# MoE slots per expert cut from 640 to 624 in a fused attention and mixture-of-experts kernel

## Chip, cores and metric

One Trainium2 chip, one core, one launch. The metric is the device time of the launch in microseconds, as the median of the runs shown. TensorE is called PE, VectorE DVE, ScalarE ACT, GpSimd POOL and SyncE SP, as in the profile.

## What is computed

The reference is rotary attention on 4 sequences of 576 tokens with 8 heads of 64, whose output becomes 2304 rows of 512, followed by a mixture of 8 experts with two experts per row:

```python
logits = x @ w_gate
noise_scale = np.log1p(np.exp(x @ w_noise))
noisy_logits = logits + noise_scale * noise
top2 = np.argpartition(-noisy_logits, 2, axis=1)[:, :2]
# top2_w: softmax over the two chosen logits
for e in range(E):
    for k in range(2):
        mask = top2[:, k] == e
        h = np.maximum(x[mask] @ w1[e], 0.0)               # 512 -> 1024
        out[mask] += top2_w[mask, k, None] * (h @ w2[e])   # 1024 -> 512
```

There are 2304 x 2 = 4608 pairs of row and expert, 576 per expert on average. How many an expert gets depends on the data.

## The kernel before

**Routing and slots.** Attention runs first. As its rows become ready, the gate picks two experts for each, and POOL scatters every row with its number and its two shares into a DRAM tensor `xs_rows` (lines 1066 to 1083). There each expert has a region of `REG` rows, of which the first `CAP` = 640 are its static slots (line 29). Slots that no row takes hold zeros and a row number `FAR` past the output, which the last scatter drops. All 8 experts are then computed over all 640 slots, so the static program does not depend on the counts. `count` (lines 1323 to 1341) compares the largest count with `CAP` on the device; if it is larger, a branch at the end (lines 1485 to 1501) reloads that expert's weights and handles the rest in blocks of 128 rows (`more`, line 1431).

**One expert.** `load_x` (line 1172) transposes the expert's slots into `xt`, 128 partitions by 8 chunks by 640 columns (four chunks of the high half of each value and four of the low half), and loads the row numbers and shares (`meta`). `up` (line 1210) makes one of 8 blocks f of 128 hidden features: 12 products over all slots (4 chunks by 3 combinations of high and low parts), which for 640 columns are issued as two matmuls of 320 columns each, 24 in all. ACT writes the high half of the ReLU into `hid` (`hh`, line 1238) and DVE the low half (`hl`, line 1236). `down` (line 1278) makes the output of one tile j of 128 slots with 24 matmuls of 512 columns, whose weights are slices of `hid`. DVE scales the result by the share and adds the rows gathered before (`y`, line 1302), and POOL scatters the sum into the output (line 1309). `fetch` (line 1259) gathers those rows after all scatters of the expert before have landed.

**The first two experts** are split at slot 256 (`EARLY`, line 1164). Their first 256 slots are worked on while the last rows are still being routed, with up matmuls of 256 columns; the other 384 slots follow with up matmuls of 384 columns. Experts 2 to 7 use `FULL`.

**Buffers.** The up blocks use three PSUM buffers `ps`, the down tiles two buffers `dn`. There are two `xt`, one `hid` for even and one for odd experts, one set of `w1` and of `w2` for each parity, three staging buffers for weights, two `y` and six `prev`. Weights are loaded in 8 pieces per expert by SP and split into high and low halves by ACT (line 1135) and DVE (line 1137).

**Order.** A list scheduler in the program (`Plan.order`, line 199) puts every engine's work into one fixed order before anything is emitted. It takes each step's estimated duration, dependencies and buffers, and a priority. The priority of the expert steps is a running clock `clk` that `ups` advances per up block and each down tile by 5.12 (lines 1362 to 1389), plus a table of hand-set offsets (`dp`, line 1391), one per step in the order of their creation. The steady order on PE is: up block 0 of expert e + 1, the five down tiles of expert e, up blocks 1 to 7 of expert e + 1, up block 0 of expert e + 2, and so on.

All matmuls of the attention and of the up and down blocks go through the helper `mm`, line 537.

Of the kernel before, what the change touches and what calls it, by code (L numbers as in the profile page):

```python
# [12 lines left out]
F16 = mybir.dt.float16  # L13
# [8 lines left out]
NTOK, DM, NE, FF = B * S, 512, 8, 1024  # L22
# [3 lines left out]
QS, VS, XS, MC = 16.0, 64.0, 128.0, 64.0  # L26
PB = 12
GS, W1S, W2S = 256.0, 32.0, 32.0
CAP = 640
NJ = CAP // 128  # L30
REG = NTOK + CAP
ROW = 1024 + 20
FAR = 1 << 20

# [149 lines left out]
class Plan:  # L184
# [5 lines left out]
    def add(self, name, eng, dur, fn, deps=(), prio=0.0, uses=(), port=False, land=None, after=0.0, rows=128):  # L190
        assert name not in self.by, name
        op = Op(name, eng, dur, fn, deps, prio, uses, port, land, after, rows)
        for b in op.uses:
            b.left += 1
        self.ops.append(op)
        self.by[name] = op
        return name
# [114 lines left out]
def build(ctx, tc, q, k, v, w_gate, w_noise, noise, w1, w2, tab_d, out):  # L312
    nc = tc.nc
    xs = nc.dram_tensor("xs_rows", (NE * REG, ROW // 2), I32, kind="Internal").ap()

# [10 lines left out]
    pools = {}  # L326
# [209 lines left out]
    def mm(o, w, m, first, last):  # L536
        nc.tensor.matmul(o, w, m, start=first, stop=last, skip_group_check=True)  # L537
# [275 lines left out]
    def masks():  # L813
        nc.gpsimd.iota(cst["t1"], pattern=[[1, 128]], base=0, channel_multiplier=-1)
        nc.gpsimd.iota(cst["t2"], pattern=[[-1, 8], [1, 8]], base=0, channel_multiplier=0)
        nc.gpsimd.iota(cst["t3"], pattern=[[REG, 8]], base=0, channel_multiplier=0)
        nc.gpsimd.iota(cst["t4"], pattern=[[1, 8]], base=0, channel_multiplier=0)
# [33 lines left out]
    def fill_rows(e, part):  # L851

        j0, j1, c = ((3, NJ, 0), (0, 3, 512))[part]
        nc.scalar.dma_start(xs[e * REG + 128 * j0:e * REG + 128 * j1, c:522].rearrange("(j p) m -> p j m", p=128),
                            pad[:, None, c:522].to_broadcast([128, j1 - j0, 522 - c]))
# [32 lines left out]
    def ring(name, bufs):  # L888
        if name not in R_:
            R_[name] = Ring(name, bufs, lambda: None)  # L890
        return R_[name]
# [218 lines left out]
    hid = {}  # L1110
# [52 lines left out]

    EARLY = ((0, 256), (256, CAP))
    FULL = ((0, CAP),)

    def tiles_of(c0, c1):
        return range(c0 // 128, c1 // 128)

    xbuf, mbuf, gbuf, hbuf, pbuf, ybuf = {}, {}, {}, {}, {}, {}  # L1170

    def load_x(e, c0, c1, deps, pr):
        def f():
            s = hid.setdefault(e, dict(meta={}, gsc={}, prev={}, adds=[]))
            if e == 0 and c0 == 0:
                xt = pools["r"].tile([128, 8, c1], F16, name="xe")
            else:
                if "xt" not in s:
                    s["xt"] = pools["l"].tile([128, 8, CAP], F16, name="xt", bufs=2)
                xt = s["xt"][:, :, c0:c1]  # L1180
            s["xt", c0] = xt
            rows = xs[e * REG + c0:e * REG + c1]
            nc.sync.dma_start_transpose(out=xt, in_=rows[:, 0:512].bitcast(F16))  # L1183
            n = (c1 - c0) // 128
            meta = pools["r"].tile([128, NJ, 10], I32, name="meta", bufs=4)
            nc.sync.dma_start(meta[:, 0:n], rows[:, 512:522].rearrange("(j p) m -> p j m", p=128))
            for j in tiles_of(c0, c1):
                s["meta"][j] = (meta, j - c0 // 128)

        def weigh():  # L1190
            s = hid[e]
            n = (c1 - c0) // 128
            meta = s["meta"][c0 // 128][0]
            gsc = pools["r"].tile([128, NJ], F32, name="gsc", bufs=4)
            nc.vector.tensor_scalar(gsc[:, 0:n], meta[:, 0:n, e].bitcast(F32), 1.0 / (XS * W1S * W2S), None, op0=OP.mult)
            for j in tiles_of(c0, c1):
                s["gsc"][j] = gsc[:, j - c0 // 128:j - c0 // 128 + 1]
        if e == 0 and c0 == 0:
            xbuf[e, c0] = Buf(ring("xe", 1))
        else:  # L1200
            if (e, "xt") not in xbuf:
                xbuf[e, "xt"] = Buf(ring("xt", 2))
            xbuf[e, c0] = xbuf[e, "xt"]
        mbuf[e, c0], gbuf[e, c0] = Buf(ring("meta", 4)), Buf(ring("gsc", 4))
        n = (c1 - c0) // 128
        add(("x", e, c0), "SP", 1.1 * n + .4, f, deps=deps + ["swap_right"] + ([] if e == 0 and c0 == 0 else ["swap_left"]),
            uses=[xbuf[e, c0], mbuf[e, c0]], prio=pr, land=1.25 * n + .2)
        add(("wei", e, c0), "DVE", .2, weigh, deps=[("x", e, c0)], uses=[mbuf[e, c0], gbuf[e, c0]], prio=pr + 3)

    def up(e, f, c0, c1, pr):  # L1210
        n = 2 if c1 - c0 > 512 else 1
        w_ = (c1 - c0) // n
        ps_ = Buf(bigs)

        def mms():
            s = hid[e]
            wh, wl = wt[e]["w1"]
            xt = s["xt", c0]
            ps = ps_().rearrange("p (a b) -> p a b", a=2)
            i = 0  # L1220
            for c in range(4):
                for w, x in ((wh, c), (wh, 4 + c), (wl, c)):
                    for a in range(n):
                        mm(ps[:, a, 0:w_], w[:, c, f * 128:(f + 1) * 128], xt[:, x, a * w_:(a + 1) * w_], i == 0, i == 11)
                    i += 1

        def cut(lo):
            s = hid[e]
            if "hh" not in s:
                hid_ = pools["l" if e % 2 else "r"].tile([128, 2, 8, CAP], F16, name="hid", bufs=1)  # L1230
                s["hh"], s["hl"] = hid_[:, 0], hid_[:, 1]
            ps = ps_().rearrange("p (a b) -> p a b", a=2)
            hh = s["hh"][:, f, c0:c1].rearrange("p (a b) -> p a b", a=n)
            if lo:
                hl = s["hl"][:, f, c0:c1].rearrange("p (a b) -> p a b", a=n)
                nc.vector.scalar_tensor_tensor(hl, ps[:, 0:n, 0:w_], 0.0, hh, op0=OP.max, op1=OP.subtract)  # L1236
            else:
                nc.scalar.activation(hh, ps[:, 0:n, 0:w_], AF.Relu)  # L1238
        if e not in hbuf:
            hbuf[e] = Buf(ring("hid%d" % (e % 2), 1))  # L1240
        w = c1 - c0
        a, d = {256: (.28, .33), 384: (.39, .47), 640: (.6, .74)}[w]
        add(("up", e, f, c0), "PE", 12 * w / 2400 + .06, mms, deps=[("x", e, c0)] + wdone[e, "w1"],
            uses=[xbuf[e, c0], wbuf[e, "w1"], ps_], prio=pr)
        add(("hh", e, f, c0), "ACT", a, lambda: cut(False), deps=[("up", e, f, c0)] + (["swap_left"] if e % 2 else ["swap_right"]),
            uses=[ps_, hbuf[e]], prio=pr)
        add(("hl", e, f, c0), "DVE", d, lambda: cut(True), deps=[("hh", e, f, c0)], uses=[ps_, hbuf[e]], prio=pr)

    def ids(e, j, a):
# [9 lines left out]
    def fetch(e, j, pr):  # L1259
# [7 lines left out]
        if e:  # L1267
            before_ = [("sp", e - 1, i) for i in (range(2) if e == 1 and j < 2 else range(NJ))]
            if e == 1 and j >= 2:
                before_ += [("sp", 0, i) for i in range(NJ)]  # L1270
        if e == 0:
# [6 lines left out]
    def down(e, j, pr, prev=True):  # L1278
# [27 lines left out]
        def spread():  # L1306
# [10 lines left out]
        add(("sp", e, j), "POOL", 1.07, spread, deps=[("y", e, j)] + ([("zero", i) for i in range(18)] if e == 0 else []) +  # L1317
            ([("sp", e - 1, i) for i in range(NJ)] if e and not (e == 1 and j < 2) else []),
            uses=[yb, mbuf[e, c0]], prio=pr - 2, land=1.4)
# [3 lines left out]
    def count():  # L1323
# [13 lines left out]
        t = cst["tail"] = rp.tile([128, NE], I32, name="tails")  # L1337
        nc.gpsimd.iota(t, pattern=[[REG, NE]], base=0, channel_multiplier=1)
        V.tensor_tensor(t, t, cnt[:, 0:NE], op=OP.add)
# [5 lines left out]
    wdone[0, "w2"] = plan_weights(0, "w2", O["w20"], 4, [])  # L1345
    wdone[1, "w1"] = plan_weights(1, "w1", O["w11"], 4, [])
    load_x(0, *EARLY[0], put0, M0 - 30)
    load_x(1, *EARLY[0], put0, M0 - 29)
    for f in range(8):
        up(0, f, *EARLY[0], M0 + f)  # L1350
# [3 lines left out]
    for f in range(8):  # L1354
        up(1, f, *EARLY[0], M0 + 11 + f)
# [4 lines left out]
    for e in range(2):  # L1360
        load_x(e, *EARLY[1], put0 + put1 + put2, -10)
    clk = [M0 + 40]

    def go(us):
        clk[0] += us

    def ups(e, f):
        up(e, f, *(FULL[0] if e > 1 else EARLY[1]), clk[0])
        go(3.2 if e > 1 else 1.95)

    for f in range(8):
        ups(0, f)
# [58 lines left out]
    def more(e, r0, late):  # L1431
        pl, pr = pools["l"], pools["r"]
        xt = pl.tile([128, 8, 128], F16, name="xt_m", tag="xt", bufs=2)
        meta = pr.tile([128, 10], I32, name="meta_m", tag="meta", bufs=4)
        rows = xs[e * REG + r0:e * REG + r0 + 128] if late else xs[bass.ds(r0 + e * REG, 128)]
        nc.sync.dma_start_transpose(out=xt, in_=rows[:, 0:512].bitcast(F16))
# [100 lines left out]
```

## Time and profile before

| | |
|---|---|
| median of 3 runs | 772.33 us (770.82, 772.33, 772.92) |
| span of the profiled execution | 772.6 us |
| own time of the profiled execution | not given apart from its span |
| PE busy | 723.6 us, 94% of the span |
| DVE, ACT, POOL busy | 415.1, 286.5, 363.9 us |
| stretch in which PE works on experts without a pause | 358.8 to 764.5 us |

The span is the time from the first to the last instruction of one execution. Matmul records are pipelined: a row's mean duration of one matmul contains the pipe's filling, so the pace of a stream of matmuls is read by dividing a gapless stretch by its count, not from the mean of one.

### The profile page before, as it was taken

What the parts mean: (1) busy time and instruction counts of PE and PEld (TensorE: products, weight loads), DVE (VectorE), ACT (ScalarE), POOL (GpSimd) and SP (SyncE); (2) the same over time, 40 slices, a digit from 0 to 9 for tenths busy, and PEclk for the clock granted to TensorE, in tenths of its full rate; (3) what the DMA queues carried; (4) which work ended last, traced back from release to release, by engine and by line L of the source; (5) the groups of instructions that cost most, each with busy time, mean ns of one, the idle gap of its engine ahead of it and who ended that gap; (6) DMA issues with size and microseconds to landing.
All of it is one profiled execution on the core that took longest, in us unless ns stands there. A gap on an engine that the chain in (4) does not pass through costs nothing.

```text
span 772.6 us, 18628 instructions
## 1 busy us (share of the span) xinstructions
PE 723.6 (94%) x8094; PEld 497.5 (64%) x8094; DVE 415.1 (54%) x649; ACT 286.5 (37%) x435; POOL 363.9 (47%) x317
## 2 busy tenths in 40 slices
PE   4899998999888899989999999999999999999995
PEld 3677777788777777878555567466475574664752
DVE  6758779877769778777224524334343352342211
ACT  2543546555554665764112313213223042140100
POOL 5799797996515697826431212240331222302311
PEclk9999999999799999999999999999999999999998
DMA  7786565957427594587744894645535537431201
GB/s 156 145 154 127 118 146 122 184 127 157 96 56 170 185 245 117 152 189 258 213 129 146 152 244 136 189 163 144 167 132 165 152 112 194 146 117 55 79 29 39
DMA packets 178812, 112.15 MB, mean 145 GB/s; under 512 B 150431, under 2 KB 155039, under 8 KB 178720
## 3 DMA queue, kind: packets, MB, share of 16 engines
q1 hardware_dynamic: 161632, 72.72, 42.8%
q0 software_dynamic: 9120, 29.03, 10.8%
q10 hardware_dynamic: 7968, 9.12, 3.5%
q8 instruction: 65, 1.06, 0.6%
q14 instruction: 27, 0.22, 0.1%
HBM read 58.57 MB, written 29.22 MB: 114 GB/s over the span
## 4 chain that ended last, share of the span: by engine, by line
PE 51%; issue 11%; DVE 5%; POOL 5%; ACT 4%; DMA 4%; SPq 1%; POOLq 0%; ACTq 0%; DVEq 0%
PE ps L537 25%; PE dn L537 20%; PE acc L537 6%; ACT p L662 2%; POOL p L673 2%; DVE nm L562 2%; POOL out_dram L1309 1%; DMA prev<-out_dram,meta 1%; DMA out_dram<-y,meta 1%; POOL prev L1263 1%; POOL xs_rows L1071 1%; ACT ps L662 1%; ACT xr L778 1%; SPq L1183 1%; DMA xs_rows<-xr,r_ii 1%
## 5 line engine op out<-in xcount | busy, mean ns | idle before, releaser
L537 PE MATMUL dn<-w2h,hid 128*128 128x512 f16 x640 | 191.8, 379 | 0.0
L537 PE MATMUL ps<-xt,w1h 128*128 128x320 f16 (+2 forms) x960 | 177.6, 301 | 0.3 <-DVE nf L1330 0.3
L1309 POOL DMA_INDIRECT out_dram<-y,meta x40 | 53.3, 1332 | 251.7 <-DVE y L1302 209.2
L537 PEld LDWEIGHTS <-hid 128*128 128x128 f16 x960 | 93.9, 98 | 111.9
L1238 ACT ACTIVATE hid<-ps 128x640 f16<-128x640 f32 (+2 forms) x80 | 47.7, 598 | 216.7 <-PE ps L537 216.7
L537 PEld LDWEIGHTS <-w1h 128*128 128x128 f16 x1024 | 100.0, 98 | 41.4 <-issue 0.9
L537 PE MATMUL dn<-w2l,hid 128*128 128x512 f16 x320 | 121.3, 379 | 0.0
L673 POOL TENSOR_TENSOR p<-p 128x1152 f16<-128x1152 f32 (+1 forms) x48 | 100.5, 2108 | 33.3 <-ACT p L662 33.0
L537 PE MATMUL ps<-xt,w1l 128*128 128x320 f16 (+2 forms) x480 | 113.0, 301 | 0.0
L1236 DVE SCALAR_TENSOR_TENSOR hid<-ps,hid 128x640 f16<-128x640 f32 (+2 forms) x80 | 54.9, 690 | 104.6 <-ACT hid L1238 104.5
L662 ACT ACTIVATE p<-ps,pbias 128x576 f32<-128x576 f32 x112 | 79.6, 741 | 72.5 <-PE ps L537 70.8
L562 DVE TENSOR_REDUCE nm<-ps 128x2 f32<-128x576 f32 x128 | 91.2, 750 | 26.2 <-PE ps L537 25.8
L1302 DVE SCALAR_TENSOR_TENSOR y<-dn,gsc,prev 128x512 f32<-128x512 f32 x38 | 28.5, 750 | 135.2 <-PE dn L537 126.0
L537 PE MATMUL ps<-qt,kt 64*128 64x288 f16 (+5 forms) x1200 | 84.9, 262 | 8.4 <-DVE p L669 2.5
L537 PE MATMUL acc<-vb,p 128*128 128x65 f16 (+3 forms) x2040 | 78.1, 194 | 9.5 <-DVE xr L776 8.2
L537 PEld LDWEIGHTS <-p 128*128 128x128 bf16 (+3 forms) x2040 | 70.4, 98 | 22.2 <-issue 17.6
L537 PE MATMUL ps<-kt,qt 64*128 64x288 f16 (+1 forms) x960 | 80.5, 290 | 4.2 <-DVE nm L562 0.9
L537 PEld LDWEIGHTS <-kt 64*128 64x128 f16 (+1 forms) x1200 | 54.1, 97 | 22.4 <-issue 14.1
L537 PEld LDWEIGHTS <-w1l 128*128 128x128 f16 x512 | 50.1, 98 | 19.5
L537 PEld LDWEIGHTS <-qt 64*128 64x128 f16 (+1 forms) x960 | 46.4, 98 | 21.2 <-issue 11.3
L1263 POOL DMA_INDIRECT prev<-out_dram,meta x38 | 39.3, 1034 | 44.1 <-DMA out_dram<-y,meta 25.8
L1071 POOL DMA_INDIRECT xs_rows<-xr,r_ii x36 | 38.5, 1070 | 45.1 <-DVE xr L1054 23.4
(137 smaller groups left out, 810.7 us busy)
## 6 DMA issues: line engine op xcount, KB each, us to landing
wst<-in_moe_w_dram SPq DMA_DIRECT2D x64, 512.0 KB, 4.1
out_dram<-pad ACTq DMA_DIRECT2D x18, 256.0 KB, 2.3
xs_rows<-pad ACTq DMA_DIRECT2D x8, 522.0 KB, 3.9
qin<-in_q_dram SPq DMA_DIRECT2D x16, 256.0 KB, 4.6
qin<-in_k_dram SPq DMA_DIRECT2D x16, 256.0 KB, 4.1
vin<-in_v_dram SPq DMA_DIRECT2D x16, 256.0 KB, 3.7
out_dram<-y,meta POOLq DMA_INDIRECT x40, 4.7
prev<-out_dram,meta POOLq DMA_INDIRECT x38, 3.8
```

Source lines behind the costliest of these rows:

```text
L537: nc.tensor.matmul(o, w, m, start=first, stop=last, skip_group_check=True)
L562: nc.vector.tensor_reduce(nm()[:, u, :, h], x, axis=AX.X, op=OP.max, negate=True)
L662: nc.scalar.activation(x if way[u] == "P" else halves(whole(u), u, h), x, AF.Exp, bias=pbias, scale=0.125 / (QS * QS))
L673: E.tensor_tensor(b, whole(u), a, op=OP.subtract)
L778: nc.scalar.copy(to, xx)
L1071: i = nc.gpsimd.indirect_dma_start(out=xs, out_offset=bass.IndirectOffsetOnAxis(ap=h["ii"][:, t, a:a + 1], axis=0), in_=r[:, slot(t)], in_ ...
L1183: nc.sync.dma_start_transpose(out=xt, in_=rows[:, 0:512].bitcast(F16))
L1236: nc.vector.scalar_tensor_tensor(hl, ps[:, 0:n, 0:w_], 0.0, hh, op0=OP.max, op1=OP.subtract)
L1238: nc.scalar.activation(hh, ps[:, 0:n, 0:w_], AF.Relu)
L1263: nc.gpsimd.indirect_dma_start(out=prev, out_offset=None, in_=out, in_offset=bass.IndirectOffsetOnAxis(ap=ids(e, j, 1), axis=0))
L1302: nc.vector.scalar_tensor_tensor(y, dn(), s["gsc"][j], s["prev"][j], op0=OP.mult, op1=OP.add)
L1309: i = nc.gpsimd.indirect_dma_start(out=out, out_offset=bass.IndirectOffsetOnAxis(ap=ids(e, j, 0), axis=0), in_=yt[0], in_offset=None, boun ...
```

## The change

`CAP` becomes 624, which is 4 x 128 + 112. `NJ`, the number of down tiles, is rounded up and stays 5; `REG` stays 2944, so the regions, loads of x, gathers and scatters keep their shapes. The up blocks of experts 2 to 7 issue two matmuls of 312 columns for each product, and those of experts 0 and 1 in their second part one of 368 in place of 384. ACT and DVE read and write 624 or 368 columns there. `hid` keeps 640 columns, and a DVE memset writes zeros into the last 16, once per expert, ahead of that expert's first low half. The estimated durations in the scheduler's tables follow. The threshold of the branch at the end becomes 624.

```diff
--- before.py
+++ after.py
@@ -26,9 +26,9 @@
 QS, VS, XS, MC = 16.0, 64.0, 128.0, 64.0
 PB = 12
 GS, W1S, W2S = 256.0, 32.0, 32.0
-CAP = 640
-NJ = CAP // 128
-REG = NTOK + CAP
+CAP = 624
+NJ = -(-CAP // 128)
+REG = NTOK + NJ * 128
 ROW = 1024 + 20
 FAR = 1 << 20
 
@@ -1165,23 +1165,24 @@
     FULL = ((0, CAP),)
 
     def tiles_of(c0, c1):
-        return range(c0 // 128, c1 // 128)
+        return range(c0 // 128, -(-c1 // 128))
 
     xbuf, mbuf, gbuf, hbuf, pbuf, ybuf = {}, {}, {}, {}, {}, {}
 
     def load_x(e, c0, c1, deps, pr):
+        n = -(-(c1 - c0) // 128)
+
         def f():
             s = hid.setdefault(e, dict(meta={}, gsc={}, prev={}, adds=[]))
             if e == 0 and c0 == 0:
                 xt = pools["r"].tile([128, 8, c1], F16, name="xe")
             else:
                 if "xt" not in s:
-                    s["xt"] = pools["l"].tile([128, 8, CAP], F16, name="xt", bufs=2)
-                xt = s["xt"][:, :, c0:c1]
+                    s["xt"] = pools["l"].tile([128, 8, NJ * 128], F16, name="xt", bufs=2)
+                xt = s["xt"][:, :, c0:c0 + 128 * n]
             s["xt", c0] = xt
-            rows = xs[e * REG + c0:e * REG + c1]
+            rows = xs[e * REG + c0:e * REG + c0 + 128 * n]
             nc.sync.dma_start_transpose(out=xt, in_=rows[:, 0:512].bitcast(F16))
-            n = (c1 - c0) // 128
             meta = pools["r"].tile([128, NJ, 10], I32, name="meta", bufs=4)
             nc.sync.dma_start(meta[:, 0:n], rows[:, 512:522].rearrange("(j p) m -> p j m", p=128))
             for j in tiles_of(c0, c1):
@@ -1189,7 +1190,6 @@
 
         def weigh():
             s = hid[e]
-            n = (c1 - c0) // 128
             meta = s["meta"][c0 // 128][0]
             gsc = pools["r"].tile([128, NJ], F32, name="gsc", bufs=4)
             nc.vector.tensor_scalar(gsc[:, 0:n], meta[:, 0:n, e].bitcast(F32), 1.0 / (XS * W1S * W2S), None, op0=OP.mult)
@@ -1202,7 +1202,6 @@
                 xbuf[e, "xt"] = Buf(ring("xt", 2))
             xbuf[e, c0] = xbuf[e, "xt"]
         mbuf[e, c0], gbuf[e, c0] = Buf(ring("meta", 4)), Buf(ring("gsc", 4))
-        n = (c1 - c0) // 128
         add(("x", e, c0), "SP", 1.1 * n + .4, f, deps=deps + ["swap_right"] + ([] if e == 0 and c0 == 0 else ["swap_left"]),
             uses=[xbuf[e, c0], mbuf[e, c0]], prio=pr, land=1.25 * n + .2)
         add(("wei", e, c0), "DVE", .2, weigh, deps=[("x", e, c0)], uses=[mbuf[e, c0], gbuf[e, c0]], prio=pr + 3)
@@ -1227,11 +1226,13 @@
         def cut(lo):
             s = hid[e]
             if "hh" not in s:
-                hid_ = pools["l" if e % 2 else "r"].tile([128, 2, 8, CAP], F16, name="hid", bufs=1)
-                s["hh"], s["hl"] = hid_[:, 0], hid_[:, 1]
+                hid_ = pools["l" if e % 2 else "r"].tile([128, 2, 8, NJ * 128], F16, name="hid", bufs=1)
+                s["hh"], s["hl"], s["hid"] = hid_[:, 0], hid_[:, 1], hid_
             ps = ps_().rearrange("p (a b) -> p a b", a=2)
             hh = s["hh"][:, f, c0:c1].rearrange("p (a b) -> p a b", a=n)
             if lo:
+                if CAP % 128 and "rest" not in s:
+                    s["rest"] = nc.vector.memset(s["hid"][:, :, :, CAP:], 0.0)
                 hl = s["hl"][:, f, c0:c1].rearrange("p (a b) -> p a b", a=n)
                 nc.vector.scalar_tensor_tensor(hl, ps[:, 0:n, 0:w_], 0.0, hh, op0=OP.max, op1=OP.subtract)
             else:
@@ -1239,7 +1240,7 @@
         if e not in hbuf:
             hbuf[e] = Buf(ring("hid%d" % (e % 2), 1))
         w = c1 - c0
-        a, d = {256: (.28, .33), 384: (.39, .47), 640: (.6, .74)}[w]
+        a, d = {256: (.28, .33), 368: (.38, .45), 624: (.585, .72)}[w]
         add(("up", e, f, c0), "PE", 12 * w / 2400 + .06, mms, deps=[("x", e, c0)] + wdone[e, "w1"],
             uses=[xbuf[e, c0], wbuf[e, "w1"], ps_], prio=pr)
         add(("hh", e, f, c0), "ACT", a, lambda: cut(False), deps=[("up", e, f, c0)] + (["swap_left"] if e % 2 else ["swap_right"]),
@@ -1366,7 +1367,7 @@
 
     def ups(e, f):
         up(e, f, *(FULL[0] if e > 1 else EARLY[1]), clk[0])
-        go(3.2 if e > 1 else 1.95)
+        go(3.12 if e > 1 else 1.87)
 
     for f in range(8):
         ups(0, f)
```

## Rows read from the trace of the kernel before

**Rows 1.** The page: busy time by engine, and TensorE's granted clock in 40 slices.
```profile
PE 723.6 (94%) x8094; PEld 497.5 (64%) x8094; DVE 415.1 (54%) x649; ACT 286.5 (37%) x435; POOL 363.9 (47%) x317
...
PEclk9999999999799999999999999999999999999998
```

**Rows 2.** Busy time by stage; behind POOL stand granted clock, DMA share, GB/s.
```profile
437.00:452.60 15.60, 15.60 (x75) 7.08 (x73) 4.49 (x6) 2.49 (x3) 2.16 (x4) 1.00 1.18 186
...
507.80:533.90 26.10, 26.10 (x194) 18.79 (x192) 12.56 (x13) 8.71 (x11) 7.27 (x7) 1.00 0.38 122
...
764.50:772.60 8.10, 0.00 (x0) 0.00 (x0) 0.75 (x1) 0.00 (x0) 0.99 (x1) 0.75 0.08 26
```

**Rows 3.** What PE waited for, 330 to 772.6 us: total, times, longest.
```profile
PE ps L537 <- DVE hid L1236: 0.8, 2, 0.5
...
PE ps L537 <- DVE nf L1330: 0.3, 1, 0.3
```

**Rows 4.** The chain that ended last: start, duration, engine and tile, count of instructions.
```profile
390.31 21.45 PE ps L537 x132
...
427.29 9.75 PE ps L537 x60
...
452.58 29.34 PE ps L537 x216
481.92 25.90 PE dn L537 x120
507.82 26.08 PE ps L537 x192
```

**Rows 5.** Groups by form, 385 to 772.6 us: busy us, mean ns.
```profile
L537 PEld LDWEIGHTS <-w1h 128*128 128x128 f16 x896 | 87.7, 98 | 38.6
...
L1236 DVE SCALAR_TENSOR_TENSOR hid<-ps,hid 128x640 f16<-128x640 f32 x48 | 39.6, 824 | 87.1 <-ACT hid L1238 87.1
...
L1137 DVE SCALAR_TENSOR_TENSOR w1l<-wst,w1h 128x1024 f16<-128x1024 f32 x24 | 29.2, 1221 | 6.5 <-ACT w1h L1135 5.3
...
L1135 ACT ACTIVATE w1h<-wst 128x1024 f16<-128x1024 f32 x24 | 25.2, 1053 | 37.4 <-DMA wst<-in_moe_w_dram 36.1 <-PE ps L537 1.3
```

**Rows 6.** DVE groups by form, the whole span: the two memsets there are.
```profile
L797 DVE MEMSET tmx<- 128x320 uint32 x2 | 0.7, 325 | 0.2
L805 DVE MEMSET cm<- 2x128 f16 x2 | 0.3, 165 | 0.1
```

**Rows 7.** DVE in order of time: first low halves, `cnt`, a steady-state last weight piece, `meta`.
```profile
350.23 0.75 DVE L1236 SCALAR_TENSOR_TENSOR hid<-ps,hid 128x256 f16<-128x256 f32 x2
...
357.54 0.17 DVE L1336 CAST cnt<-nf 128x11 int32<-128x11 f32 x1
...
449.31 0.41 DVE L1195 TENSOR_SCALAR gsc<-meta 128x5 f32<-128x5 f32 x1 [0.50 <-DMA meta<-xs_rows]
...
522.58 1.23 DVE L1137 SCALAR_TENSOR_TENSOR w1l<-wst,w1h 128x1024 f16<-128x1024 f32 x1
```

**Rows 8.** The chain of waits inside 336 to 372 us.
```profile
357.08 0.96 POOL xs_rows L1071
358.04 0.16 POOL tails L1338
...
358.24 0.17 DVE tails L1339
358.40 0.34 DVE hid L1236
```

**Rows 9.** SP's queue in order of time: the load of expert 2's x.
```profile
431.24 12.99 SPq L1183 DMA_TRANSPOSE xt<-xs_rows  x1
```

**Rows 10.** DMA issues of the whole span: count, KB each, median us to landing.
```profile
wst<-in_moe_w_dram SPq DMA_DIRECT2D x64, 512.0 KB, 4.1
...
out_dram<-y,meta POOLq DMA_INDIRECT x40, 4.7
...
xt<-xs_rows SPq DMA_TRANSPOSE x9, 6.8
```

## The prediction

> **What bounds the kernel now.** I began with the page: PE is busy for 94% of the span and its granted clock is near full in every slice [rows 1]. That average covers the attention as well, so I asked for the busy time by stage from the first expert on. In every stage between 358.8 and 764.5 us PE is busy for the whole stage at a granted clock of 1.00, which is 2.4 GHz; DVE, ACT and POOL are each busy for about half of it or less, and only behind 764.5 us, in the last scatter, does PE stand still [rows 2]. The list of what PE waited for says the same from the other side: for the up blocks and the count there are three short waits, of 0.8 us and 0.3 us in all [rows 3], and the full stages leave no room for one behind 358.8 us [rows 2]. The chain of waits therefore runs through PE alone in this stretch, in alternating pieces of up blocks and down tiles [rows 4]. Whatever shortens a matmul there shortens the end, as long as what PE needs next is there sooner too.
>
> **What one column is worth.** The pieces of the chain have no gap, so duration over count is the pace. A matmul of 320 columns takes 26.08 / 192 = 135.8 ns, one of 384 columns 9.75 / 60 = 162.5 ns (21.45 / 132 gives the same), one of 512 columns 25.90 / 120 = 215.8 ns [rows 4]. From 320 to 512 that is 80.0 ns for 192 columns, 0.4167 ns each, one column per cycle at 2.4 GHz, with a remainder of 2.4 ns in each matmul. From 320 to 384 it is 26.7 ns for 64, the same again.
>
> The Trainium skill, page "TensorE: Matmul & The Clock Gate", section "Back-to-back issue gap", says otherwise for streams in which every matmul brings its own weight load, as here: about 81 ns at 128 columns and 131 ns at 512, which is 0.13 ns a column. By that, as an estimate from the page, the change would give 1.6 us in place of 5.1. The trace does not agree: its 512 columns take 215.8 ns with a weight load each. The mechanism stays as a rival below.
>
> **The sum.** Experts 2 to 7 have 8 up blocks of 24 matmuls each: 6 x 8 x 24 = 1152, and each loses 8 columns, 3.33 ns: 3.84 us. Experts 0 and 1 have 2 x 8 x 12 = 192 matmuls in their second part, and each loses 16 columns, 6.67 ns: 1.28 us. Together -5.12 us. No row shows 312 or 368 columns. From below the bound is no gain at all, if the engine streamed in coarser steps; from above, all of a matmul's time shrinks in proportion: 1152 x 135.8 x 8/320 + 192 x 162.5 x 16/384 = 5.2 us. I take 5.12, since three widths lie on one line. The weight load does not become the bound: it takes 98 ns [rows 5], and the shorter matmul 132.5.
>
> The matmuls of the down tiles, the gathers, the scatters, the loads of x and their descriptors are as many and as long as before: 0.
>
> ACT and DVE read 2.5% fewer columns. They are off the path, so this counts 0. They are also what frees the three PSUM buffers of the up blocks: a block is 24 x 132.5 ns = 3.18 us now, and DVE needs 0.82 for its low half and at most one weight piece of 1.22 beside it [rows 5], 2.0 us.
>
> **The memset** is new: one per expert, 256 values per partition in 16 runs, on DVE ahead of the expert's first low half. Behind it in DVE's queue stand that low half and, through the PSUM buffer that it frees, PE. The nearest rows are 0.165 us for 128 values and 0.325 us for 320 words of 4 bytes [rows 6], so 0.17 to 0.33 us, and I take 0.25; less than nothing is excluded, since nothing is removed for it. Six of the eight fall in the full up blocks, where DVE has 1.1 us to spare in each: 0, and if that cover were gone, 6 x 0.33 = 2.0 us. The other two come together, since the first low halves of experts 0 and 1 run as a pair at 350.23 us [rows 7], in the one stretch where PE still waits for DVE. There the chain goes through POOL's scatters of routed rows, whose next issue is at 357.08, to the `tails` at 358.04 and on DVE at 358.24, and only then to the low half that releases PE at 358.79 [rows 8]. DVE's own input for that point, `cnt`, is ready at 357.71 [rows 7], 0.5 us earlier. So the two memsets cost between 0 and 0.66 us; half a microsecond of delay goes into that slack, and I take 0.1.
>
> **What PE could now wait for.** PE runs ahead by 1.28 us up to expert 2 and by 0.64 us more with each expert. Most of its suppliers run on the same clock: weight pieces, casts and gathers stand in queues whose steps wait for PE's own releases. A typical last piece of `w1` ends at 523.8 us [rows 7], and the first block that uses it starts 3.26 us before 533.9, at 530.6: 6.8 us to spare, of which a period takes at most 0.64. The tight place is expert 2's first up block at 452.58. Its x is issued by SP at 431.24, takes until 444.2 there [rows 9], and `meta`, which stands behind it in the queue, has landed when DVE starts on it at 449.31 [rows 7]; the DMA engines are fully taken in this stretch (share 1.18) [rows 2]. So at least 3.3 us are left. PE comes 1.28 us earlier, while the load follows the 11 early up blocks ahead of expert 0's down tiles, which are 0.88 us earlier: 0.4 us of the 3.3 go. I count 0. The scheduler may order some steps anew, as its estimates change by 2%; the order of up blocks within an expert is free, and a later x is the case just named.
>
> **The sum and its base.** 772.6 - 5.12 + 0.1 = 767.6 us for the profiled execution, whose own time is not given. The median of the runs is 0.3 below its span, so 767.3. Runs of the same kernel spread from 770.82 to 772.92, about 0.3%; less than that (2.3 us) cannot be told from no change.
>
> **Rivals.**
>
> *Late data at expert 2.* With the DMA engines full between 431 and 457 us, x of expert 2 or a gather lands as late as before or later, and PE waits at 452.58: the 1.28 us of the first two experts are given back, 768.6 us. For it speaks the DMA share, against it the 3.3 us.
>
> *Width does not pay in full.* A matmul of 312 columns costs as much as one of 320; then the change does not do what it says, and only the memsets show, 772.4. Or the pace belongs to the pair of matmul and weight load, and the 98 ns of the load [rows 5] do not shrink: then only (135.8 - 98) / 135.8 = 28% of the 5.12 us come, 1.4, which gives 771.0. Against both speak the three widths on one line; for the first only that no row of an up block or a down tile has a width that isn't a multiple of 32. The section of the Trainium skill named above ("TensorE: Matmul & The Clock Gate", "Back-to-back issue gap") speaks for the second and would make it 770.7.
>
> *Slower: a count above 624.* The threshold of the branch moves too. If any expert gets 625 rows or more, the end of the kernel reloads that expert's 8 weight pieces and works on a further block of 128. The trace shows 40 scatters, 8 x 5 [rows 10], so no count was above 640; it cannot tell 625 to 640 from less. The reference's routing of its own inputs gives 624, 578, 567, 542, 540, 557, 608 and 592, so the largest count is exactly at the threshold, and the test is "greater than". One more row for expert 0 decides it; the nearest such row misses by 0.0008 in its logit, far more than the high and low halves lose. The price: 8 pieces, at least 8 x 1.22 us of casts [rows 5] and at most 8 x (4.1 + 1.05 + 1.22) with no overlap [rows 5, 10], x 6.8 [rows 10], 96 short matmuls at the 98 ns of their weight loads, 24 of 215.8 ns, and a scatter of 4.7 [rows 10]: between 36 and 77 us. With three staging buffers the pieces overlap in part; I take 45, which gives about 812 us.
>
> **How the numbers follow.** Forecast 0.80 (767.3), late data 0.10 (768.6), width 0.06 (771.0 or 772.4), overflow 0.04 (812). The first two are faster by over 0.3%, that is below 770.0; the third is within it, the fourth slower: 0.90, 0.06, 0.04. The range covers the first two with the runs' spread of about 1 us: 766.2 to 769.6; width and overflow are left out.
>
> **What would show it.** In the profile after, up stretches should have a pace of 132.5 ns (24 matmuls in 3.18 us, 192 in 25.44) and 155.8 ns for 368 columns, and down stretches 215.8 as before. PE should have no new wait behind 358.8 us, the eight memsets should take 0.17 to 0.33 us each, and the last scatter should stay 8.1 us behind PE's end. I am wrong if 312 columns take more than 134 ns, if PE waits at expert 2's first block, or if scatters beyond 40 appear.

## The result and the profile after

The changed kernel takes 766.12 us (median of four runs, 764.91 to 766.88) beside 772.62 us for the kernel before: a ratio of 0.9919 with a 95% interval of 0.9896 to 0.9943, or 4.4 to 8.0 us less. The forecast was 767.3 us, in a range of 766.2 to 769.6. So the sign and the size hold. The median lies 1.2 us below the forecast, 0.1 us below the lower end of the range. The profiled execution took 765.78 us, with a span of 763.9: about 1.9 us lie around the span. (The profiled execution of the kernel before had a span of 772.6, so by the same 1.9 us it took more than the median shown for it.)

The chain that ended last in the profile after, from expert 0's second up blocks on (start, duration, engine and tile, count):

```profile
386.33 20.57 PE ps L537 x132
406.90 15.54 PE dn L537 x72
422.44 9.35 PE ps L537 x60
431.79 12.95 PE dn L537 x60
444.74 3.18 PE ps L537 x24
447.92 2.59 PE dn L537 x12
450.51 25.44 PE ps L537 x192
475.95 25.90 PE dn L537 x120
```

Against [rows 4], every piece has shrunk by what its columns are worth: 21.45 to 20.57, 9.75 to 9.35, 26.08 to 25.44, and the down tiles stay at 25.90. That is 25.44 / 192 = 132.5 ns for 312 columns and 9.35 / 60 = 155.8 ns for 368. One thing is new: expert 2's first up block (24 matmuls) now stands between the first and the second half of expert 1's last down tile, where before all 72 down matmuls came first.

The last scaled tile of the kernel starts at 764.50 us in the first profile of the kernel before and at 755.41 here. I use the stretch from the start of expert 0's second up blocks to that point as the ruler in what follows, since it holds all matmuls that the change touches and little else. The two rows of DVE in order of time, before and after:

```profile
764.50 0.75 DVE L1302 SCALAR_TENSOR_TENSOR y<-dn,gsc,prev 128x512 f32<-128x512 f32 x1 [4.43 <-PE dn L537]
755.41 0.75 DVE L1303 SCALAR_TENSOR_TENSOR y<-dn,gsc,prev 128x512 f32<-128x512 f32 x1 [4.43 <-PE dn L537]
```

The ruler lasts 764.50 - 390.31 = 374.19 us before and 755.41 - 386.33 = 369.08 after: 5.11 us less, where the column sum is 5.12. From its end to the end of the span it is 8.1 us before and 8.5 after.

The new DVE memsets in the groups by form, which answer to [rows 6]:

```profile
L1235 DVE MEMSET hid<- 128x128 uint32 x8 | 1.3, 165 | 0.0
```

Eight of 0.165 us, at the lower end of the bound; the row shows them as 128 words of 4 bytes.

The spans differ by 8.7 us: 5.1 on the ruler, 4.0 ahead of it (390.31 - 386.33), and 0.4 the other way behind it. Ahead of the experts both programs issue the same work in the same order. In both, PE has little to do around 199 us, and its granted clock then falls. The busy time by stage, whose column after POOL's is the granted clock, for the kernel before:

```profile
196.00:200.00 4.00, 2.51 (x46) 1.96 (x40) 3.74 (x10) 3.51 (x7) 2.52 (x2) 1.00 0.24 49
200.00:204.00 4.00, 3.04 (x40) 3.03 (x39) 3.94 (x4) 2.60 (x3) 3.02 (x2) 0.73 0.67 148
204.00:208.00 4.00, 4.00 (x30) 2.88 (x30) 2.70 (x4) 1.16 (x2) 1.58 (x1) 0.50 0.98 206
208.00:212.00 4.00, 4.00 (x48) 3.48 (x49) 0.93 (x2) 0.85 (x2) 1.26 (x1) 0.50 0.29 56
```

and for the profile after:

```profile
196.00:200.00 4.00, 1.74 (x30) 1.41 (x30) 3.84 (x7) 3.88 (x8) 1.69 (x1) 1.00 0.25 49
200.00:204.00 4.00, 3.86 (x50) 3.40 (x51) 3.72 (x3) 1.76 (x3) 3.85 (x2) 0.70 0.84 192
204.00:208.00 4.00, 4.00 (x66) 3.32 (x63) 2.69 (x3) 2.00 (x3) 1.29 (x2) 0.88 1.10 202
208.00:212.00 4.00, 4.00 (x92) 3.40 (x90) 2.84 (x4) 1.00 (x2) 1.54 (x2) 1.00 0.06 12
```

At 0.50, which is 1.2 GHz, PE gets through about half as much: 204 to 212 us hold 78 matmuls before and 158 after. In the first profile of the kernel before, the low clock lasts until 212, in the one after it is gone by 206. As an estimate, a granted clock of c over 4 us of busy PE loses 4 (1 - c) us, 5.1 us before (200 to 212) and 1.7 after: about 3.4 us. The same steps on either side of this stretch, two rows of the kernel before and then two of the profile after, bear that out:

```profile
200.96 1.13 PE L537 MATMUL acc<-vb,p 128*128 128x65 f16 x30 [1.77 <-DVE xr L776]
216.48 1.42 DVE L562 TENSOR_REDUCE nm<-ps 128x2 f32<-128x576 f32 x2 [1.05 <-PE ps L537]
...
200.14 1.09 PE L537 MATMUL acc<-vb,p 128*128 128x65 f16 x30 [1.77 <-DVE xr L776]
212.54 1.42 DVE L562 TENSOR_REDUCE nm<-ps 128x2 f32<-128x576 f32 x2 [1.05 <-PE ps L537]
```

The profile after is 0.82 us ahead in front of the low clock and 3.94 behind it, so 3.1 of the 4.0 us arise there.

### The profile page after: what moved, and what is told of

Its sections match the earlier page's. It is cut to its first block, busy times and chain, and to the rows that moved or that the text cites. A ratio compares the mean times of both kernels' runs of the same rounds, so it can differ in the third digit from the quotient of the medians.

```text
span 763.9 us, 18636 instructions
## 1 busy us (share of the span) xinstructions
PE 715.4 (94%) x8094; PEld 494.9 (65%) x8094; DVE 416.3 (54%) x657; ACT 284.9 (37%) x435; POOL 362.3 (47%) x317
## 4 chain that ended last, share of the span: by engine, by line
PE 54%; issue 10%; DVE 6%; POOL 4%; ACT 4%; DMA 2%; SPq 0%; POOLq 0%; DVEq 0%; ACTq 0%
PE ps L537 26%; PE dn L537 20%; PE acc L537 6%; ACT p L662 2%; POOL p L673 2%; DVE nm L562 2%; POOL out_dram L1310 1%; DMA prev<-out_dram,meta 1%; POOL prev L1264 1%; ACT xr L778 1%; DVE xr L776 1%; ACT ps L662 1%; DMA out_dram<-y,meta 1%; DMA gt<-xr 1%; PE ps L956 1%
## 5 line engine op out<-in xcount | busy, mean ns | idle before, releaser
L537 PE MATMUL ps<-xt,w1h 128*128 128x312 f16 (+2 forms) x960 | 173.9, 298 | 0.3 <-DVE nf L1331 0.3
L1310 POOL DMA_INDIRECT out_dram<-y,meta x40 | 50.3, 1258 | 255.5 <-DVE y L1303 214.9
L1239 ACT ACTIVATE hid<-ps 128x624 f16<-128x624 f32 (+2 forms) x80 | 46.7, 585 | 238.0 <-PE ps L537 238.0
L537 PE MATMUL ps<-xt,w1l 128*128 128x312 f16 (+2 forms) x480 | 111.5, 298 | 0.0
L1237 DVE SCALAR_TENSOR_TENSOR hid<-ps,hid 128x624 f16<-128x624 f32 (+2 forms) x80 | 53.8, 674 | 105.0 <-ACT hid L1239 104.9
L1264 POOL DMA_INDIRECT prev<-out_dram,meta x38 | 41.2, 1084 | 36.3 <-DMA out_dram<-y,meta 20.1
```

The costliest lines, as they stand in the source:

```text
L1264: nc.gpsimd.indirect_dma_start(out=prev, out_offset=None, in_=out, in_offset=bass.IndirectOffsetOnAxis(ap=ids(e, j, 1), axis=0))
L1310: i = nc.gpsimd.indirect_dma_start(out=out, out_offset=bass.IndirectOffsetOnAxis(ap=ids(e, j, 0), axis=0), in_=yt[0], in_offset=None, boun ...
```

## The experiments

The question was whether the gain is the column sum, 5.1 us, and the further 1.4 us are chance, or whether the new order, the memsets or something ahead of the experts has a part in it.

**The kernel before, and the changed kernel, once more.** No edit.

> The kernel before once more, unchanged. Theory A (the 1.4 us that the measured gain has beyond the forecast's sum, and the 4 us by which the profiled run before reached its first expert later, are chance: how long PE's granted clock stays at 0.50 after PE's stop at 199 to 201 us): ratio to the kernel before 1.000 within 0.2%; in this run's profile the stretch 202 to 214 us shows a low clock for some other length than the first profile's 10 us, and the expert stretch from the first uninterrupted up block to the last down tile again lasts 405.7 us. Theory B (something in the code ahead of the experts is slower before): the first expert is again reached at about 358.8 us.

> The changed kernel once more. Theory A: over more rounds the gain closes in on the column sum, 5.1 us (ratio 0.9934), and the expert stretch lasts 405.7 - 5.1 = 400.6 us. Theory B: it stays at 6.5 us or more (ratio 0.9916), and the first expert is reached about 4 us sooner than in the repeated kernel before.

On the chip of these runs all kernels, the one before too, took 1 to 2% longer and spread over some 20 us, so the times can't tell 5 us apart: the kernel before against itself gave 0.9974 (0.9921 to 1.0026), the changed kernel 0.9983 (0.9939 to 1.0027). Taken at its word that interval would leave out both 5.1 and 6.5 us. The profiles can tell. The expectations name a stretch of 405.7 us that begins with the first uninterrupted up blocks; in the repeat of the kernel before PE pauses among these, so I read the ruler, which begins behind them. The ruler of the kernel before is 777.10 - 402.90 = 374.20 us, the same to 0.01. Its granted clock is low for about 3.5 us around 204 us, not 10; and the changed kernel's profile shows 1.00 from 196 to 220 us and falls only behind that. In a later profile of the changed kernel the low clock lasts about 10 us there. The changed kernel in this repeat, and then in the later one:

```profile
200.00:204.00 4.00, 4.00 (x63) 3.59 (x60) 4.00 (x4) 2.02 (x4) 4.00 (x2) 1.00 0.94 214
204.00:208.00 4.00, 4.00 (x90) 3.40 (x91) 3.90 (x5) 1.21 (x2) 1.82 (x2) 1.00 1.23 146
...
200.00:204.00 4.00, 4.00 (x33) 3.36 (x32) 2.79 (x1) 0.81 (x2) 3.79 (x2) 0.50 0.93 207
204.00:208.00 4.00, 4.00 (x36) 3.52 (x33) 2.69 (x3) 2.00 (x3) 0.69 (x1) 0.50 0.92 170
```

So the length of the low clock varies between executions of one program. It is about 10 us in one of two profiles of the kernel before, and in two of four of the changed kernel. The repeated kernel before reached its first down tile at 379.2 us, 10 us later than in its first profile, and the changed kernel at 375.8: what lies ahead of the experts differs by more than the change is worth, in both.

The ruler of the changed kernel is 766.29 - 396.64 = 369.65 us here, 0.57 more than in its first profile, and the list of what PE waited for has an entry, 0.4 us, that is in neither of the first two: x of expert 2. The forecast named that place as a rival.

**The old order.** Only the estimates that the scheduler sees are put back:

```diff
-        a, d = {256: (.28, .33), 368: (.38, .45), 624: (.585, .72)}[w]
-        add(("up", e, f, c0), "PE", 12 * w / 2400 + .06, mms, deps=[("x", e, c0)] + wdone[e, "w1"],
-        go(3.12 if e > 1 else 1.87)
+        a, d = {256: (.28, .33), 368: (.39, .47), 624: (.6, .74)}[w]
+        add(("up", e, f, c0), "PE", 12 * {256: 256, 368: 384, 624: 640}[w] / 2400 + .06, mms, deps=[("x", e, c0)] + wdone[e, "w1"],
+        go(3.2 if e > 1 else 1.95)
```

> The change with the scheduler's estimates put back to those of 640 slots, so that PE, ACT, DVE, POOL and SP work in the order of the kernel before (expert 2's first up block behind expert 1's last down tile, not inside it). If the new order is worth nothing: the same time as the changed kernel within 0.2%, and the expert stretch 400.6 us. If part of the gain is the new order: slower than the changed kernel by that part, up to 1.4 us (767.5 where the changed kernel has 766.1).

> The changed kernel again, beside the same with the old order: in the profile the expert stretch from the first uninterrupted up block to the last down tile lasts 400.6 us if x of expert 2 is there in time, and longer by PE's wait for it if not. Theory A: the gain over the kernel before is 5.1 us within what the runs can tell; theory B: 6.5 us or more.

> The change in the order of the kernel before, again. If the new order (expert 2's first up block half a down tile earlier) is worth nothing: as the changed kernel within 0.2%. If it costs where x of expert 2 is late: PE waits in the changed kernel for x and not in this one, and this one is faster by that wait, 0 to 2.6 us. If the new order is worth something: this one slower by up to 1.4 us.

> The changed kernel again, for its time over many rounds. Theory A (the column sum and nothing else): 5.1 us faster than the kernel before, ratio 0.9934; theory B: 6.5 us or more, 0.9916.

> The change in the order of the kernel before, for its time over many rounds beside the changed kernel. From the profiles so far: 0 to 0.6 us faster than the changed kernel, the wait for expert 2's x, so the same within what the runs can tell; from expert 0's second up blocks to the last down tile the profile shows the time of the kernel before less 5.12 us.

The ratios to the kernel before: 0.9918 (0.9877 to 0.9959), 0.999 (0.9945 to 1.0034) and 0.993 (0.9901 to 0.9959) for the old order, 0.9983 (0.9942 to 1.0024) and 0.9919 (0.9895 to 0.9943) for the changed kernel. The last of each is from another, quieter chip: 766.95 us for the old order and 766.0 for the changed kernel beside 773.11. The intervals overlap, so the times don't rank the two orders. The ruler does. In the old order it is 761.15 - 392.07 = 369.08 us in the last profile, and 369.08 and 369.07 in the other two, though these executions took 770.98, 793.09 and 791.39 us; in the changed kernel it is 369.65, 369.60 and 370.85 in the three repeats. What the three have in common is a piece of the chain, here of the last repeat:

```profile
427.85 3.94 PE ps L537 x26
431.79 19.91 DMA xt<-xs_rows
451.71 0.05 issue
451.75 3.35 PE ps L537 x24
455.11 2.59 PE dn L537 x12
457.70 25.44 PE ps L537 x192
```

with the only wait that PE has in the expert stretch of that profile (in us, times, longest):

```profile
PE ps L537 <- DMA xt<-xs_rows: 1.6, 1, 1.6
```

PE stands at expert 2's first up block, 24 matmuls, until x has landed; SP issued it at 431.79. In the old order the same place reads

```profile
437.54 15.54 PE dn L537 x72
453.07 28.62 PE ps L537 x216
```

with no such wait, although SP issued x at 432.13 there, no sooner: 40.06 us behind the start of the ruler, as in the last repeat of the changed kernel (40.05). The new order puts the block 12 down matmuls, 2.59 us, earlier, and that uses up what was spare. SP's queue in the first profile of the changed kernel and in the last of the old order, and x on the chain of the other two repeats:

```profile
426.39 13.73 SPq L1185 DMA_TRANSPOSE xt<-xs_rows  x1
432.13 14.67 SPq L1185 DMA_TRANSPOSE xt<-xs_rows  x1
...
436.70 18.70 DMA xt<-xs_rows
443.84 18.66 DMA xt<-xs_rows
```

From the issue of x to the block there are 444.74 - 426.39 = 18.35 us in the new order and 453.07 - 432.13 = 20.94 in the old. From issue to landing x takes 18.7, 18.7 and 19.9 us in the three repeats, too long for the first and short enough for the second; in the first profile of the changed kernel it came in time. Why that duration differs between executions is open. The new order costs 0 in the first profile and 0.5 to 1.8 us in the repeats, and gains nothing in any.

**The memset eight times.**

```diff
-                    s["rest"] = nc.vector.memset(s["hid"][:, :, :, CAP:], 0.0)
+                    for _ in range(8):
+                        s["rest"] = nc.vector.memset(s["hid"][:, :, :, CAP:], 0.0)
```

> The memset of the last 16 columns issued eight times per expert in place of once, 64 in all, 56 more. At 0.165 us each that is up to 1.3 us ahead of each expert's first low half. If the memsets are hidden as forecast: nothing in experts 2 to 7, and in the early stretch of experts 0 and 1, where there is 0.5 us of slack, up to 14 x 0.165 = 2.3 us less the slack, about 1 to 1.8 us. If none of it is hidden: 56 x 0.165 = 9 us.

The ratio to the kernel before, 0.9983 (0.9935 to 1.0031), tells nothing on that chip. In the full up blocks nothing is lost: the ruler is 770.70 - 401.46 = 369.24 us, 0.16 above the undisturbed 369.08, and those 0.16 stand at expert 2's first block. The early stretch is another matter. DVE in order of time:

```profile
356.90 0.18 DVE L1025 TENSOR_SCALAR r_sel<-r_rk 128x40 f16<-128x40 f32 x1
357.05 1.97 DVE L1236 MEMSET hid<- 128x128 uint32 x8
358.94 0.36 DVE L1238 SCALAR_TENSOR_TENSOR hid<-ps,hid 128x256 f16<-128x256 f32 x1
359.28 1.97 DVE L1236 MEMSET hid<- 128x128 uint32 x8
```

Eight in a row take 1.97 us, so they start 0.26 us apart and not 0.165. What they delay on DVE is `cnt`. The start of `r_sel` in the kernel before (its `cnt` stands in [rows 7]), `r_sel` and `cnt` in the changed kernel, and `cnt` here:

```profile
350.13 0.18 DVE L1025 TENSOR_SCALAR r_sel<-r_rk 128x40 f16<-128x40 f32 x1
...
346.33 0.18 DVE L1025 TENSOR_SCALAR r_sel<-r_rk 128x40 f16<-128x40 f32 x1
353.91 0.17 DVE L1337 CAST cnt<-nf 128x11 int32<-128x11 f32 x1
...
368.10 0.17 DVE L1338 CAST cnt<-nf 128x11 int32<-128x11 f32 x1
```

From `r_sel` to `cnt` it is 7.41 us before, 7.58 in the changed kernel and 368.10 - 356.90 = 11.20 here. So the two memsets of the change cost DVE 0.17 us, and the 14 more 3.6 us, 0.26 each. How much of that reaches PE can't be read so finely, because the point at which PE resumes also waits for POOL [rows 8]. From `r_sel` to the start of the 96 up matmuls ahead of expert 0's down tiles it is 368.97 - 356.90 = 12.07 us here. In the kernel before it is 358.79 - 350.13 = 8.66 and in its repeat 10.07, in the four profiles of the changed kernel 8.48, 9.75, 10.70 and 9.47. Against the changed kernel the 14 memsets thus cost PE 1.4 to 3.6 us, where 1 to 1.8 were expected, and a cost of 0.17 us by the two cannot be seen.

**576 slots in the up blocks.**

```diff
-CAP = 624
+CAP = 576
...
-    V.tensor_scalar(nf[:, 8:9], nf[:, 8:9], float(CAP), None, op0=OP.is_gt)
+    V.tensor_scalar(nf[:, 8:9], nf[:, 8:9], 640.0, None, op0=OP.is_gt)
...
```

The branch itself also compares with 640, and the scheduler's estimates follow the widths.

> The up blocks work on 576 slots: two matmuls of 288 columns in experts 2 to 7, one of 320 in the second part of experts 0 and 1; the memset zeros the last 64 columns of hid, and the branch's threshold is 640. The rows in slots 576 to 639 of experts 0, 1, 6 and 7 are left out. By the column law (0.4167 ns a column + 2.4 ns a matmul) a matmul of 288 columns takes 122.4 ns, one of 320 135.8, and the gain on the kernel before is 1152 x 13.33 ns + 192 x 26.67 ns = 20.5 us. If the weight load of 98 ns is part of the pace, the 288-column matmul takes about 132 ns and the gain is about 6 us. If x of expert 2 keeps its place in time, PE waits for it: the first two experts are 5.1 us shorter and only 3.3 us were spare, so 2 to 3 us of the 20.5 are given back.

The time was 761.98 us beside 784.92 (ratio 0.9739, 0.9665 to 0.9814). In the chain

```profile
436.86 6.52 PE ps L537 x48
443.38 15.54 PE dn L537 x72
458.92 23.52 PE ps L537 x192
```

23.52 / 192 = 122.5 ns for 288 columns and 6.52 / 48 = 135.8 for 320, and the ruler is 755.48 - 401.76 = 353.72 us, 20.47 less than before, where the column law gives 20.48. The rival with the weight load in the pace (about 6 us) is out. The wait for x that I expected did not come: this program kept all 72 down matmuls ahead of expert 2, and its x took 5.7 us in SP's queue in place of 13.

**608 slots, so that the branch runs.**

```diff
-CAP = 624
+CAP = 608
...
```

Here too the estimates follow.

> The change one step further, 608 slots, so that expert 0's 624 rows go over the threshold and the branch at the end runs for it: reload of 8 weight pieces and one further block of 128 rows. Columns: 1152 x 6.67 ns + 192 x 13.33 ns = 10.2 us gained. The branch: 45 us (36 to 77) by the working of the prediction. Together 35 us slower than the kernel before (26 to 67). If the branch were nearly free, the kernel would be about 10 us faster than before.

848.4 us beside 784.92, ratio 1.0823 (1.0728 to 1.0918). By stage, from expert 7's down tiles to the end:

```profile
700.00:774.40 74.40, 74.40 (x415) 40.41 (x413) 16.58 (x20) 10.27 (x13) 15.87 (x23) 1.00 0.20 66
774.40:811.20 36.80, 12.51 (x120) 9.14 (x120) 13.61 (x19) 8.56 (x14) 5.26 (x4) 0.72 0.37 112
811.20:849.00 37.80, 0.00 (x0) 0.00 (x0) 0.00 (x0) 0.00 (x0) 0.00 (x0) 0.52 0.04 10
```

Behind the last scaled tile of the static part, at 774.44 us, the kernel runs for 74.6 us in place of 8.1 [rows 2], so by the profile the branch costs 66 us: 37 for the reload and the block of 128 rows, and 38 less the usual tail in which no engine computes anything. The times say somewhat more: 63.5 us slower, with the 10.2 gained about 74, and 67 to 82 by the interval. By the profile the bound of 36 to 77 held. The 45 that I took has no term for the second half, and what the launch does in it was not found out.

## Why the prediction was right, and where it was off

*The worth of a column* was right to the hundredth. Six widths now lie on one line: 288, 312, 320, 368, 384 and 512 columns take 122.5, 132.5, 135.8, 155.8, 162.5 and 215.8 ns, that is 0.4167 ns a column and 2.4 to 2.5 ns more. Both forms of the rival "width does not pay in full" are ruled out by measurement. (One of that rival's times, 770.7, left out the 0.1 us of the memsets and should have been 770.8.) The ruler gives 5.11 us of the 5.12, in the first profile and, within 0.02, in all three of the old order.

*The memsets* were forecast at 0.17 to 0.33 us each and 0.1 us in all; they took 0.165. In the full blocks they cost nothing: the ruler shows the column sum with them. For the early pair DVE's `cnt` comes 0.17 us later, which the spread at PE hides. The reason given, that half a microsecond of delay goes into the slack of `cnt` against `tails`, rests on one execution: those 0.5 us were a wait for POOL, and in the changed kernel's first profile `tails` follows `cnt` with no wait for POOL (354.23 behind 353.91). So the 0.1 us was neither confirmed nor refuted; it was small enough not to matter.

*What PE could now wait for* is the step that failed in part. I counted the scheduler's new order as nothing, and gave expert 2's x 3.3 us, of which PE would use 0.4. The order that came out moves that block 2.59 us earlier besides, so about 0.3 us were left, and in three of four profiles x was late, by 0.5 to 1.8 us on the ruler. The 3.3 us themselves were those of one execution. A wait at this block was one of my signs of being wrong, and by it I was wrong in these three. It is the rival "late data at expert 2", at its place and near its price (1.28 us), but only in part by its reason: x is issued 0.87 us earlier on the ruler (40.06 in place of 40.93), as forecast, and with the same issue the old order shows no wait, so it is the order that takes the spare time. That the profile of the first runs shows no wait was luck. The wait doesn't decide the time. (The 444.2 that I read from [rows 9] is the end of SP's work on the issue, not the landing: in the last repeat these are 448.2 and 451.7. The bound by `meta` was sound.)

*The overflow* did not come about: 40 scatters and no reload in the profile after, so 624 is enough for these data, with nothing to spare. The test is "greater than", so one row more would decide it; no run had 625. The run with 608 slots, which expert 0's 624 rows exceed, shows the price: 66 us or somewhat more, not 45.

*The time itself.* The measured gain is 6.5 us in the first runs and 0.9919 again in the last, against 5.0 forecast; both intervals reach down to 4.4 us and include 5.1. Among the last runs the fastest are 769.12 us before and 764.22 after, 4.9 us apart; among the first they are 5.9 apart. The expert stretch explains 3.3 to 5.1 us, depending on expert 2's x, and the stretch of low clock near 200 us accounts for 3.1 of the 4.0 us by which the two first profiles differ ahead of it. What the median has beyond the column sum, 1.4 us, is not shown to come from the change. The long low clock occurs in both kernels, so chance is the likelier reason, but with so few profiles its frequency in each was not settled. The old order, with 0.993, sits on the column sum.

## What to carry to other kernels

Where PE ran without a pause here, at 288 to 512 columns, a matmul's cost was its columns and 2.5 ns, and trimming padding from the moving side paid to the hundredth of a microsecond, also at widths that are no multiple of 32; divide a gapless stretch by its count to price it. When a program orders its own work from estimated durations, changing the estimates is a change of its own: keep the old ones in a second variant and compare the order around the tightest transfer. Take a limit as low as the data allow only with the price of crossing it at hand.

## What was not expected of the hardware

After one and the same thin spot in PE's work at about 199 us, the granted clock stayed at 1.2 GHz for anything between nothing and 10 us, in executions of programs that are identical up to that point. Memsets of 0.165 us into the same part of one tile follow each other every 0.26 us. And after the branch at the end, the launch went on for 37.8 us with no engine computing and little on the DMA queues (10 GB/s).
